# A smaller first query load, one expert unit regrouped to two output products, and a new hand-written order in an attention-and-expert kernel on one core

## The chip, the cores and the metric

The kernel runs on one core of a Trainium2 chip. The metric is the device time of one execution in microseconds. Five engines work side by side, each through its own queue in order: TensorE (PE, matmuls; its weight loads are listed as PEld), VectorE (DVE), ScalarE (ACT), GpSimd (POOL) and SyncE (SP), which issues nearly all DMAs here.

## What is computed

The first half is linear attention with sketched features, for 4 batches, 4 heads, 1088 positions and head size 32; its output, turned to 4352 tokens of 128 values, goes through an expert layer with a rational function in the place of an activation.

```python
def phi(x):
    a = np.einsum('rd,bhsd->bhsr', S1, x)          # r = 8
    b = np.einsum('rd,bhsd->bhsr', S2, x)
    return np.einsum('bhsi,bhsj->bhsij', a, b).reshape(*x.shape[:-1], r * r)
kv = np.einsum('bhsf,bhsd->bhfd', phi(k), v);  z = np.sum(phi(k), axis=2)
x = (phi(q) . kv) / (phi(q) . z + 1e-06)           # -> [4352, 128]
h = x @ w_in                                       # d_ff = 2048
P = a[0] + a[1]*h + a[2]*h*h + a[3]*h*h*h
Q = 1.0 + abs(b[0])*abs(h) + abs(b[1])*h*h
out = (P / (Q + 1e-06)) @ w_out
```

## The kernel before

**Tiling.** Keys are handled by batch (K0 to K3), each in two parts. Queries are handled in pieces of a batch (Q0.0 to Q3.2; 256 to 384 tokens each). The expert layer is cut into 21 units: each is a stretch of 256 or 512 tokens and 4, 8 or 16 of the 16 blocks of 128 hidden values, so a unit is 1024, 2048 or 4096 wide in the free dimension (all of units 3 to 17 are 4096 wide, unit 20 is 1024).

**A unit's stages.** H: matmuls h = w_in x into a PSUM tile of 1024 (two buffers). E: ACT copies it to bf16 (`hh`, three buffers). U, W, Y on DVE: |h|, |b1||h| + |b0|, and their product. P: the linear factor a3 h + a2, in halves of 2048, on ACT (`.a`) or DVE (`.d`). V on DVE: times h, which gives `g` = a3 h h + a2 h. L and X on ACT, in pieces of 2048: ln of 1 + 1e-6 + Y, and exp of its negative, which is the reciprocal `r`. S on DVE: s = h r. G on DVE: g = g s. Then three sums of output matmuls, all into one PSUM tile of a stretch: Or (w_out times a0, with r), Os (w_out times a1, with s) and Og (w_out, with g). ST transposes the finished tile on DVE, and OUT stores it. The three scaled copies of w_out are made at the start (w0 to w5, in halves).

**A query piece's stages.** T (DVE transpose), sk (sketch matmuls), c (copy out of PSUM), dw and dr (SP writes the sketches to DRAM and reads them back spread over partitions; Q0.0 and Q0.1 do without), f (DVE product), p (matmuls with the key sums `kvz`), pl, r, x (denominator plus 1e-6, reciprocal, quotient), b (transpose on PE) and kk (ACT copies into the ring `xT` that H reads). **A key batch's stages**: T0 to T2, s, c, f, p (products with v), k (copies into `kvz`).

**The order** is written out by hand in the string ORDER (L31 to L72); nothing else schedules the work. The loop at L600 runs through its steps and issues each one's instructions, so a step's place fixes its place in every engine's queue: I and F are loads issued by SP (I0 to I11 those of the start, F1.k, F1.q, F1.v and so on those of a later batch), Z is that many matmuls of zeros that fill PE's time, AB and SS prepare small constants.

**Loads of the start**, in `early` (L158): I0 and I1 keys of batch 0, I11 the second sketch matrix, I2 the first queries, I3 four loads of v, I8 the coefficients a and b, I7 the other queries of batch 0, I9 and I10 halves of w_out, I4 to I6 parts of w_in. **Names that the change touches**: `early` (L158), `a2, a3` (L240), `left`, the count of output matmuls still to come for a stretch (L456), `span`, the columns of a stage's piece (L464), `p` (L513) and the table `stages` (L596).

Of the kernel before, what the change touches and what calls it, by code (L numbers as in the profile page):

```python
# [36 lines left out]
Q0.1.kk.a V0.0 Y1.0 Q1.2.T S0.0 E2.1 G0.0 Or0.0 L1.0 U2.0 F1.v F2.k Q0.2.dr Q0.3.dw K1.p0 K1.p1 Q1.1.sk Og0.0
Q0.2.f K1.k0.a K1.k1.a Q0.2.p X1.0 Q1.1.c.a Q0.2.pl.a P2.0.a W2.0 K2.T0 K2.T1 Q0.2.r K2.T2 Q0.2.x F2.q Q1.0.dw
Os0.0 Or1.0 K2.s0 Q0.2.b Y2.0 K2.c0.a Q0.2.kk.a L2.0 K2.s1 Q2.0.T H3.0 K2.c1.a E3.0 K2.f0 V2.0 V1.0 S1.0 K2.f1
Q0.3.dr Q1.1.dw H3.1 Q1.2.sk Q2.0.sk H3.2 X2.0 Q1.2.c.a E3.1 Q1.0.dr H3.3 Q2.1.T S2.0 G2.0 Q0.3.f G1.0 E3.2  # L40
Q2.0.c.a E3.3 P3.0.a H4.0 Q0.3.p U3.0 E4.0 Q1.0.f Q0.3.pl.d W3.0 Q0.3.r Y3.0 P3.1.a H4.1 Q1.0.p Q1.0.pl.a E4.1
Q0.3.x Q1.0.r Q2.2.T Q1.0.x P4.0.d V3.0 Q1.2.dw Q2.0.dw F2.v Q1.1.dr F3.q F3.k Q2.1.sk Q2.1.c.a L3.0 H4.2 Q2.1.dw
Q1.2.dr H4.3 Q0.3.b E4.2 E4.3 Q0.3.kk.a X3.0 Q1.0.b Os2.0 Os1.0 K2.p0 Q1.0.kk.a K2.p1 Og1.0 H5.0 L3.1 U4.0 P4.1.d
W4.0 V4.0 Q1.1.f K2.k0.a X3.1 E5.0 K2.k1.a H5.1 E5.1 Y4.0 S3.0 Or2.0 Q1.1.p Og2.0 H5.2 L4.0 X4.0 Q1.2.f K3.T0 ST2
G3.0 K3.T1 Q3.0.T E5.2 L4.1 Q1.1.pl.a Q1.2.p H5.3 Q1.2.pl.a Q2.0.dr E5.3 X4.1 Q1.2.r P5.0.d Q1.1.r U5.0 Q1.1.x
W5.0 Q1.2.x Y5.0 S4.0 K3.T2 H6.0 H6.1 Q2.2.sk Or3.0 E6.0 H6.2 P5.1.a E6.1 Or4.0 H6.3 Or3.1 Q1.1.b Q2.2.c.a E6.2
L5.0 E6.3 P6.0.d Q2.0.f U6.0 V5.0 Og3.0 Q1.1.kk.a H7.0 X5.0 P6.1.a L5.1 E7.0 G4.0 W6.0 X5.1 Os3.0 H7.1 E7.1
Q3.0.sk Q2.0.p H7.2 Os4.0 H7.3 Q1.2.b Or4.1 P7.0.a E7.2 Q3.1.T Y6.0 Og4.0 H8.0 S5.0 Q2.0.pl.d V6.0 G5.0 Q3.2.T
Q2.2.dw OUT2 Q2.1.dr L6.0 Q2.2.dr E7.3 X6.0 P7.1.a Q3.0.c.a Q2.0.r U7.0 E8.0 ST4 Q2.0.x Q2.1.f W7.0 H8.1 Q1.2.kk.a
L6.1 E8.1 V7.0 Y7.0 OUT4 Q3.0.dw Q2.0.b H8.2 Q3.1.sk Q3.1.c.a Q3.1.dw Q3.0.dr Or5.0 Q2.1.p Q2.0.kk.a X6.1  # L50
Q2.1.pl.a E8.2 Q2.1.r S6.0 Q2.2.f P8.0.d L7.0 Or5.1 H8.3 K3.s0 K3.c0.a E8.3 Q2.1.x U8.0 G6.0 W8.0 H9.0 X7.0 Og5.0
H9.1 K3.f0 E9.0 Q2.1.b Q2.2.p Q2.2.pl.d H9.2 Y8.0 L7.1 E9.1 P8.1.a V8.0 H9.3 Os5.0 Or6.1 K3.s1 Or6.0 X7.1 E9.2
H10.0 Os6.0 P9.0.a E9.3 Og6.0 H10.1 S7.0 L8.0 P9.1.a K3.c1.a X8.0 U9.0 Q2.2.r Q2.1.kk.a E10.0 L8.1 E10.1 X8.1 F3.v
W9.0 Q3.0.f Q3.1.dr Q2.2.x K3.f1 Y9.0 ST6 G7.0 Q3.1.f H10.2 Or7.0 Or7.1 H10.3 Or8.1 Or8.0 E10.2 H11.0 L9.0 E10.3
V9.0 P10.0.d S8.0 U10.0 X9.0 E11.0 L9.1 H11.1 Os7.0 H11.2 K3.p0 E11.1 H11.3 K3.p1 X9.1 E11.2 W10.0 P10.1.d Y10.0
L10.0 E11.3 Os8.0 H12.0 K3.k1.a X10.0 K3.k0.a L10.1 X10.1 G8.0 V10.0 U11.0 S9.0 W11.0 G9.0 Q3.0.p Q3.2.sk Q2.2.b
Og7.0 H12.1 E12.0 Q3.0.pl.a Og8.0 P11.0.a E12.1 Q3.2.c.a P11.1.a S10.0 Q3.0.r Y11.0 ST8 Q3.0.x H12.2 H12.3 E12.2
L11.0 Or9.0 Q2.2.kk.a Q3.0.b Or9.1 E12.3 Q3.0.kk.a X11.0 Q3.2.dw OUT8 Q3.2.dr OUT6 G10.0 V11.0 U12.0 P12.0.d
Q3.1.p H13.0 Q3.1.pl.a L11.1 W12.0 P12.1.d Y12.0 Q3.1.r E13.0 X11.1 H13.1 Os9.0 Or10.1 H13.2 Or10.0 E13.1 L12.0
E13.2 S11.0 Q3.1.x V12.0 Q3.2.f G11.0 H13.3 H14.0 Q3.1.b Og9.0 Os10.0 X12.0 E13.3 U13.0 P13.0.d W13.0 L12.1 E14.0  # L60
X12.1 P13.1.a H14.1 E14.1 S12.0 Y13.0 Og10.0 ST10 H14.2 Q3.1.kk.a P14.0.a H14.3 Or11.0 Or11.1 E14.2 L13.0 E14.3
G12.0 V13.0 X13.0 U14.0 Q3.2.p Q3.2.pl.a P14.1.d Q3.2.r H15.0 E15.0 W14.0 Q3.2.x H15.1 L13.1 E15.1 X13.1 Or12.1
H15.2 Os11.0 H15.3 Or12.0 E15.2 Y14.0 V14.0 L14.0 S13.0 Og11.0 E15.3 U15.0 P15.0.d W15.0 P15.1.d Y15.0 X14.0 L14.1
H16.0 E16.0 Og12.0 H16.1 H16.2 Os12.0 X14.1 E16.1 L15.0 E16.2 P16.0.a V15.0 G13.0 ST12 S14.0 OUT10 OUT12 H16.3
Or13.0 Q3.2.b E16.3 Q3.2.kk.a Or13.1 H17.0 X15.0 E17.0 L15.1 Or14.0 H17.1 H17.2 E17.1 H17.3 Os13.0 Or14.1 X15.1
E17.2 U16.0.d P16.1.d W16.0.d G14.0 Y16.0 Og13.0 Os14.0 Og14.0 H18.0 V16.0 S15.0 L16.0 E17.3 U17.0.d P17.0.d
# [9 lines left out]
def kernel(  # L76
# [436 lines left out]
    def p(i, k, eng):  # L513
# [3 lines left out]
                                    op0=AX.mult, op1=AX.add)  # L517
        else:
            nc.scalar.activation(out=at(i, "g", *c), in_=at(i, "hh", *c), func=ACT.Identity, scale=a3, bias=a2)  # L519
# [123 lines left out]
```

## Time and profile before

| | us |
|---|---|
| runs before | 265.71, 266.57, 266.58; median 266.57 |
| profiled execution | 265.94 |
| its span, first to last instruction | 264.2 |
| evacuation E, 1024 wide, ACT (68) | 1.041 each |
| ln L / exp X, 2048 wide, ACT (32 / 32) | 1.955 / 1.951 each |
| factor P, 2048 wide, on ACT (16) / on DVE (16) | 2.120 / 0.806 each |
| product 4096 wide, DVE (60 in V, Y, S, G) | 2.281 to 2.291 each |
| output matmul 512 columns bf16, PE (eight in a row) | 1.73 |

A group's mean is the time from an instruction's start to its end as the profiler gives it. The next instruction of a full queue starts some 0.1 us before that end on ACT and DVE, and much earlier on PE, so means add up to more than the queue's time.

### The profile page before, as it was taken

To read this page: it belongs to the slowest core of one execution; us is meant where nothing else is said; L and a number is where in the kernel's file an instruction comes from. 1 tells how busy PE (TensorE), PEld (TensorE's weight loads), DVE (VectorE), ACT (ScalarE), POOL (GpSimd) and SP (SyncE) were. 2 spreads that over 40 slices of the span, in tenths; PEclk is the share of its full clock that TensorE was granted. 3 is DMA by queue.
4 is the path that set the end of the run, shared out by engine and by line. 5 is a ranking of instruction groups with operands and counts; after the bars stand their busy time and mean duration, and the time that the engine had idled before them with its cause. 6 is when DMAs were issued, how large, how long until landed. Compare 5 with 4: busy or idle time off the path is not lost.

```text
span 264.2 us, 3693 instructions
## 1 busy us (share of the span) xinstructions
PE 258.0 (98%) x1407; PEld 148.5 (56%) x1421; DVE 252.6 (96%) x238; ACT 242.3 (92%) x224; POOL 2.9 (1%) x24
## 2 busy tenths in 40 slices
PE   8999999999999999999999999999999999999994
PEld 3797855677344545555444655444544457465683
DVE  3899999999999999999999999999999999999993
ACT  2178998999999999999999999999999999999990
POOL 4000000000000000000000000000000000000000
PEclk9999999999999999999999999999999999999999
DMA  6999654793017104940000004600200020020121
GB/s 168 287 298 256 197 154 103 200 247 87 0 29 168 58 9 79 187 109 0 0 0 2 0 1 76 130 0 0 37 5 0 0 40 0 2 39 1 26 36 20
DMA packets 30784, 20.16 MB, mean 76 GB/s; under 512 B 20016, under 2 KB 26544, under 8 KB 30768
## 3 DMA queue, kind: packets, MB, share of 16 engines
q1 hardware_dynamic: 30080, 19.85, 30.8%
q8 instruction: 11, 0.18, 0.3%
q10 hardware_dynamic: 688, 0.08, 0.2%
q14 instruction: 5, 0.04, 0.1%
HBM read 16.71 MB, written 3.21 MB: 75 GB/s over the span
## 4 chain that ended last, share of the span: by engine, by line
PE 46%; ACT 25%; DVE 17%; issue 10%; DVEq 0%; ACTq 0%
PE h_ps L485 21%; PE out_ps L550 14%; ACT ln L528 7%; ACT r L532 6%; ACT hh L491 6%; ACT g L519 4%; DVE s L536 4%; DVE g L540 3%; PE att_ps L406 2%; DVE g L523 2%; PE out_ps L193 2%; DVE w L511 2%; PE att_ps L312 2%; DVE u L498 2%; PE att_ps L284 2%
## 5 line engine op out<-in xcount | busy, mean ns | idle before, releaser
L485 PE MATMUL h_ps<-xT,w_in_sb 128*128 128x512 f32 (+1 forms) x320 | 126.1, 533 | 0.1
L485 PEld LDWEIGHTS h_ps<-xT,w_in_sb 128*128 128x128 f32 x320 | 59.2, 190 | 43.5 <-issue 33.0
L550 PEld LDWEIGHTS <-w_out 128*128 128x128 bf16 x480 | 46.4, 98 | 48.3 <-issue 14.3
L491 ACT CAST hh<-h_ps 128x1024 bf16<-128x1024 f32 x68 | 70.8, 1041 | 1.8 <-PE h_ps L485 1.4
L528 ACT ACTIVATE ln<-w 128x2048 f32<-128x2048 bf16 (+1 forms) x36 | 66.8, 1856 | 0.4 <-DVE w L511 0.2
L532 ACT ACTIVATE r<-ln 128x2048 bf16<-128x2048 f32 (+1 forms) x36 | 66.7, 1852 | 0.4 <-PE out_ps L550 0.2
L536 DVE TENSOR_TENSOR s<-hh,r 128x4096 bf16<-128x4096 bf16 (+2 forms) x21 | 39.4, 1878 | 0.5 <-ACT r L532 0.4
L511 DVE TENSOR_TENSOR w<-w,u 128x4096 bf16<-128x4096 bf16 (+2 forms) x21 | 39.5, 1880 | 0.1
L540 DVE TENSOR_TENSOR g<-g,s 128x4096 bf16<-128x4096 bf16 (+2 forms) x21 | 39.4, 1878 | 0.1
L523 DVE TENSOR_TENSOR g<-g,hh 128x4096 bf16<-128x4096 bf16 (+2 forms) x21 | 39.5, 1882 | 0.0
L519 ACT ACTIVATE g<-hh,a_sb 128x2048 bf16<-128x2048 bf16 (+1 forms) x17 | 35.2, 2068 | 0.0
L550 PE MATMUL out_ps<-r,w_out 128*128 128x512 bf16 (+1 forms) x154 | 34.0, 346 | 0.5
L550 PE MATMUL out_ps<-g,w_out 128*128 128x512 bf16 (+1 forms) x158 | 32.6, 347 | 0.1
L550 PE MATMUL out_ps<-s,w_out 128*128 128x512 bf16 (+1 forms) x155 | 31.8, 346 | 0.3
L506 DVE TENSOR_SCALAR w<-u,b_abs 128x4096 bf16<-128x4096 bf16 (+2 forms) x19 | 22.6, 1187 | 0.1
L498 DVE TENSOR_SCALAR u<-hh 128x4096 uint16<-128x4096 uint16 (+2 forms) x20 | 21.0, 1048 | 0.3 <-ACT hh L491 0.3
L406 PEld LDWEIGHTS att_ps<-kvz,a_all 128*118 128x118 f32 (+2 forms) x144 | 16.8, 186 | 3.5 <-issue 1.3
L406 PE MATMUL att_ps<-kvz,a_all 128*118 128x66 f32 (+2 forms) x144 | 17.1, 268 | 0.1
L516 DVE TENSOR_SCALAR g<-hh,a_sb 128x2048 bf16<-128x2048 bf16 (+1 forms) x19 | 14.5, 762 | 0.2 <-ACT hh L491 0.2
L312 PEld LDWEIGHTS att_ps<-v_sb,k_p 128*64 128x64 f32 (+1 forms) x288 | 8.8, 138 | 2.4 <-issue 1.9
L278 DVE STREAM_TRANSPOSE kT<-k_sb 128x512 f32<-128x512 f32 (+2 forms) x12 | 6.2, 536 | 3.6 <-DMA k_sb<-in_k_dram 3.6
L391 DVE TENSOR_TENSOR a_all<-a_all,b_all 128x704 f32<-128x704 f32 (+3 forms) x11 | 9.7, 880 | 0.0
(58 smaller groups left out, 128.5 us busy)
## 6 DMA issues: line engine op xcount, KB each, us to landing
a_all<-sk_d SPq DMA_DIRECT2D x6, 352.0 KB
b_all<-sk_d SPq DMA_DIRECT2D x12, 176.0 KB
v_sb<-in_v_dram SPq DMA_DIRECT2D x12, 144.0 KB
k_sb<-in_k_dram SPq DMA_DIRECT2D x3, 544.0 KB
q_sb<-in_q_dram SPq DMA_DIRECT2D x3, 544.0 KB
a_all<-sk_d SPq DMA_DIRECT2D x3, 384.0 KB
b_all<-sk_d SPq DMA_DIRECT2D x6, 192.0 KB
ln<-in_moe_w_out_dram SPq DMA_DIRECT2D x2, 512.0 KB
```

The costliest lines, as they stand in the source:

```text
L406: nc.tensor.matmul(self.nd[:self.tl, o:o + 2 * KW], lhsT=self.group(t, c), rhs=kvz[self.b % 2][:, c, :], start=True, stop=True)
L485: nc.tensor.matmul(t[:, (x - part * m) * tl:(x - part * m + 1) * tl], lhsT=w_in_sb[:, (f0 + x) * 128:(f0 + x + 1) * 128], rhs=xT[:, p:p + ...
L491: nc.scalar.copy(out=at(i, "hh", c, ce), in_=live[i]["h", part][:, :ce - c])
L498: nc.vector.tensor_scalar(out=at(i, "u", *c).bitcast(U16), in0=at(i, "hh", *c).bitcast(U16), scalar1=0x7FFF, scalar2=None, op0=AX.bitwise_and)
L511: nc.vector.tensor_mul(out=at(i, "w", *c), in0=at(i, "w", *c), in1=at(i, "u", *c))
L519: nc.scalar.activation(out=at(i, "g", *c), in_=at(i, "hh", *c), func=ACT.Identity, scale=a3, bias=a2)
L523: nc.vector.tensor_mul(out=at(i, "g", *c), in0=at(i, "g", *c), in1=at(i, "hh", *c))
L528: nc.scalar.activation(out=t[:, :ce - c], in_=at(i, "w", c, ce), func=ACT.Ln, bias=1.0 + 1e-6)
L532: nc.scalar.activation(out=at(i, "r", c, ce), in_=live[i]["ln", k][:, :ce - c], func=ACT.Exp, scale=-1.0)
L536: nc.vector.tensor_mul(out=at(i, "s", *c), in0=at(i, "hh", *c), in1=at(i, "r", *c))
L540: nc.vector.tensor_mul(out=at(i, "g", *c), in0=at(i, "g", *c), in1=at(i, "s", *c))
L550: nc.tensor.matmul(outs[t0][:, :tl], lhsT=w_sb[y][:, f0 + x, :], rhs=at(i, "rsg"[y], x * tl, (x + 1) * tl), start=first and j == 0, stop=l ...
```

## The change

The first query load I2 takes 256 columns rather than 512, and I7 the other 832. For unit 6 (named in TWO) Os is left out: a1 is added to `g` ahead of the product with s, in a new stage A between V and G, one half on DVE and one on ACT. Since then g s = (a3 h h + a2 h + a1) h r, Og gives what Os and Og gave together. The last unit's pieces of L, X, S, G get a cap of 2048 (END). ORDER is new throughout. Beside the new places, these steps change engine: K0.c1, Q0.1.pl, W18, both halves of P9 and P11.1 go from ACT to DVE; Q0.3.pl, Q2.0.pl, Q2.2.pl, P6.0, P10.0, P15.1, P20, U20 and w1 go from DVE to ACT; U19 and W20 go from ACT to DVE, W19 from DVE to ACT; w4 and w5 change sides. I7 moves ahead of F1.k, I8 behind I9, I6 behind Q0.2.dw.

```diff
+QA = 256
+TWO = (6,)
+END = 2048
...
-            nc.sync.dma_start(out=q0[:, 0:512], in_=q0_src[:, 0:512])
+            nc.sync.dma_start(out=q0[:, 0:QA], in_=q0_src[:, 0:QA])
...
-            nc.sync.dma_start(out=q0[:, 512:S], in_=q0_src[:, 512:S])
+            nc.sync.dma_start(out=q0[:, QA:S], in_=q0_src[:, QA:S])
...
-    for t0, tl, f0, n in units:
-        left[t0] = left.get(t0, 0) + 3 * n
+    for i, (t0, tl, f0, n) in enumerate(units):
+        left[t0] = left.get(t0, 0) + (2 if i in TWO else 3) * n
...
-        w = WIDE.get(stage, 2048)
+        w = END if i == NU - 1 and stage in "LXSG" else WIDE.get(stage, 2048)
...
+    def plus(i, k, eng):
+        c = span(i, "P", k)
+        if eng == "d":
+            nc.vector.tensor_scalar(out=at(i, "g", *c), in0=at(i, "g", *c), scalar1=a1, scalar2=None, op0=AX.add)
+        else:
+            nc.scalar.activation(out=at(i, "g", *c), in_=at(i, "g", *c), func=ACT.Identity, bias=a1)
```

The start of the order, old and new:

```diff
-I0 I11 I1 I2 K0.T0 SS0 Z10 K0.s0 K0.T1 K0.c0.a K0.T2 K0.f0 Q0.0.T Z2 K0.s1 Z2 Q0.0.sk I3 Z2 K0.p0 I8 F1.k I7 I9 I4
-I6 I5 I10 K0.c1.a K0.f1 Q0.0.c.d Q0.0.f Q0.1.T K0.p1 K0.k1.d Q0.2.T K1.T0 K0.k0.a Q0.1.sk Q0.0.p Q0.2.sk K1.T1
+I0 I11 I1 I2 K0.T0 SS0 Z10 K0.s0 K0.T1 K0.c0.a K0.T2 Q0.0.T K0.f0 Z2 K0.s1 K0.c1.d I3 Z2 Q0.0.sk K0.p0 I7 F1.k I9
+I8 I4 I5 I10 K0.f1 K0.p1 Q0.0.c.d Q0.1.T Q0.0.f K0.k1.d Q0.2.T K1.T0 K0.k0.a Q0.1.sk Q0.0.p Q0.2.sk Q0.1.c.a
```

The part with the new stage (P6.0 and P6.1 stand before it), and the tail:

```diff
+P7.0.a U7.0.d A6.0.d W7.0.d Q3.0.f L6.1 Y7.0 E8.0 K3.c1.a K3.f1 X6.1 H8.1 Q3.1.sk Q3.1.c.a E8.1 A6.1.a S6.0 ST4
+H8.2 Q2.0.b Q2.1.p H8.3 G5.0 G6.0 Or5.0 Or5.1 Q2.2.p E8.2 P7.1.a P8.0.d Q2.0.kk.a E8.3 Q2.2.pl.a Q2.1.pl.a H9.0
...
-ST16 U19.0.a L18.0 Z1 Or17.0 E20.0 X18.0 P19.0.a W19.0.d G17.0 Y19.0 S18.0 U20.0.d L19.0 W20.0.a Os17.0 Or17.1
-Og17.0 OUT14 X19.0 OUT16 G18.0 ST17 P20.0.d Y20.0 V19.0 S19.0 V20.0 G19.0 L20.0 Z4 Or18.0 OUT17 X20.0 Og18.0
-Os18.0 Or19.0 Os19.0 Or20.0 Og19.0 S20.0 Os20.0 G20.0 Og20.0 ST20 OUT20
+Og16.0 Og15.0 H20.0 S17.0 W19.0.a L18.0 ST16 Y19.0 G17.0 E20.0 X18.0 U20.0.a L19.0 P19.0.a Z5 Or17.0 Or17.1 Os17.0
+OUT14 V18.0 S18.0 W20.0.d Og17.0 ST17 V19.0 Y20.0 X19.0 P20.0.a L20.0 S19.0 G18.0 V20.0 G19.0 OUT16 Z2 Or18.0
+OUT17 X20.0 Or19.0 Os18.0 Os19.0 Z1 Og18.0 S20.0 Or20.0 Og19.0 Os20.0 G20.0 Og20.0 ST20 OUT20
```

More of the change, by code (lines that the diff above doesn't have):

```diff
@@ L31 @@
 ORDER = """
-I0 I11 I1 I2 K0.T0 SS0 Z10 K0.s0 K0.T1 K0.c0.a K0.T2 K0.f0 Q0.0.T Z2 K0.s1 Z2 Q0.0.sk I3 Z2 K0.p0 I8 F1.k I7 I9 I4
-I6 I5 I10 K0.c1.a K0.f1 Q0.0.c.d Q0.0.f Q0.1.T K0.p1 K0.k1.d Q0.2.T K1.T0 K0.k0.a Q0.1.sk Q0.0.p Q0.2.sk K1.T1
-Q0.1.c.a Q0.0.pl.a Q0.0.r Q0.0.x K1.T2 K1.s0 Q0.2.c.a Q0.0.b K1.s1 Q0.1.f K1.c0.a Q0.3.T Q0.0.kk.a H0.0 w2.a K1.f0
-K1.c1.a AB0 w0.a K1.f1 w4.d E0.0 Q0.1.p H1.0 Q0.3.sk H2.0 Q0.2.dw F1.q Q0.1.pl.a w3.a E1.0 P0.0.d U0.0 w5.a W0.0
-Y0.0 Q0.1.r w1.d Q1.0.T P1.0.d U1.0 L0.0 Q0.3.c.d H2.1 X0.0 Q0.1.x W1.0 Q1.1.T Q1.0.sk Q1.0.c.a Q0.1.b E2.0
@@ L37 @@
[L37 to L66, printed above, removed]
@@ L67 @@
-W17.0.d Y17.0 ST14 X16.0 L16.1 P17.1.a X16.1 E18.0 H18.1 Or15.0 G15.0 V17.0 Or15.1 Os15.0 H19.0 Or16.1 L17.0 E18.1
-X17.0 P18.0.d U18.0.d S16.0 L17.1 W18.0.a V18.0 G16.0 Y18.0 Og15.0 Or16.0 Os16.0 Og16.0 H20.0 X17.1 E19.0 S17.0
-ST16 U19.0.a L18.0 Z1 Or17.0 E20.0 X18.0 P19.0.a W19.0.d G17.0 Y19.0 S18.0 U20.0.d L19.0 W20.0.a Os17.0 Or17.1
-Og17.0 OUT14 X19.0 OUT16 G18.0 ST17 P20.0.d Y20.0 V19.0 S19.0 V20.0 G19.0 L20.0 Z4 Or18.0 OUT17 X20.0 Og18.0
-Os18.0 Or19.0 Os19.0 Or20.0 Og19.0 S20.0 Os20.0 G20.0 Og20.0 ST20 OUT20
+I0 I11 I1 I2 K0.T0 SS0 Z10 K0.s0 K0.T1 K0.c0.a K0.T2 Q0.0.T K0.f0 Z2 K0.s1 K0.c1.d I3 Z2 Q0.0.sk K0.p0 I7 F1.k I9
@@ new lines @@
+I8 I4 I5 I10 K0.f1 K0.p1 Q0.0.c.d Q0.1.T Q0.0.f K0.k1.d Q0.2.T K1.T0 K0.k0.a Q0.1.sk Q0.0.p Q0.2.sk Q0.1.c.a
+Q0.0.pl.a Q0.2.c.a K1.T1 Q0.0.r Q0.0.x K1.T2 K1.s0 Q0.0.b K1.s1 K1.c0.a Q0.0.kk.a Q0.1.f K1.f0 Q0.3.T H0.0 AB0
+w0.a K1.c1.a w2.a E0.0 K1.f1 w5.d Q0.1.p H1.0 Q0.3.sk Q0.2.dw I6 F1.q w3.a w4.a Q0.1.pl.d P0.0.d U0.0 Q0.1.r V0.0
+Q0.1.x W0.0 Q0.3.c.d Y0.0 E1.0 H2.0 w1.a Q0.1.b E2.0 Q0.1.kk.a L0.0 P1.0.d Q1.0.T U1.0 Q1.1.T W1.0 V1.0 Y1.0 H2.1
+Q1.0.sk E2.1 X0.0 Q1.0.c.a F1.v K1.p0 K1.p1 Q0.2.dr Q1.2.T L1.0 U2.0 Q0.2.f Q0.3.dw F2.k Q0.2.p K1.k0.a K1.k1.a
@@ new lines @@
+Q0.2.pl.a S0.0 W2.0 G0.0 Q0.2.r Q0.2.x Q1.1.sk Or0.0 Os0.0 Q0.2.b Q1.2.sk Og0.0 X1.0 Q1.1.c.a Q0.2.kk.a P2.0.a
+Y2.0 S1.0 K2.T0 F2.q Q1.0.dw G1.0 H3.0 K2.s0 Q0.3.dr Q1.1.dw Q1.0.dr L2.0 Q1.2.c.a K2.c0.a E3.0 X2.0 K2.T1 Q2.0.T
+H3.1 Q2.0.sk K2.T2 Q2.1.T V2.0 K2.s1 K2.f0 Q2.2.T Q0.3.f H3.2 E3.1 K2.c1.a E3.2 H3.3 Q2.0.c.a E3.3 Q0.3.p H4.0
+Q0.3.pl.a P3.0.a E4.0 S2.0 K2.f1 G2.0 Q1.0.f U3.0.d Q1.2.dw Q1.1.dr F3.q F2.v Q2.0.dw F3.k Q1.2.dr Q0.3.r W3.0.d
+Q0.3.x Y3.0 Q1.0.p H4.1 H4.2 P3.1.a Q1.0.pl.a E4.1 L3.0 Q1.1.f Q1.0.r P4.0.d Q1.0.x V3.0 Q0.3.b H4.3 Os1.0 Or1.0
@@ new lines @@
+E4.2 Q0.3.kk.a E4.3 X3.0 Or2.0 Q1.0.b Q1.1.p Q2.1.sk Q1.0.kk.a Q1.1.pl.a L3.1 Q2.1.c.a X3.1 Q2.1.dw Q2.0.dr U4.0.d
+P4.1.d W4.0.d Q1.1.r Q2.2.sk H5.0 H5.1 Os2.0 Og1.0 E5.0 Q3.0.T Y4.0 Q1.1.x L4.0 E5.1 Q2.2.c.a H5.2 Q3.0.sk Og2.0
+H5.3 E5.2 Q3.0.c.a X4.0 H6.0 S3.0 Q1.2.f V4.0 G3.0 E5.3 L4.1 E6.0 X4.1 U5.0.d P5.0.d ST2 Q2.0.f W5.0.d Q2.2.dw
+S4.0 P5.1.a Y5.0 V5.0 Q1.1.b K2.p0 K2.p1 H6.1 Or3.0 H6.2 E6.1 Q1.1.kk.a P6.0.a K2.k0.a H6.3 Q1.2.p K2.k1.a Or3.1
+Q2.0.p Q3.0.dw Q2.1.dr G4.0 Q2.1.f Q3.1.T E6.2 Q1.2.pl.a L5.0 E6.3 Q1.2.r Q2.0.pl.a Q2.0.r U6.0.d X5.0 Or4.1 H7.0
@@ new lines @@
+Os3.0 K3.T0 Or4.0 H7.1 K3.s0 W6.0.d K3.T1 Q1.2.x Y6.0 Q3.2.T P6.1.a E7.0 V6.0 L5.1 OUT2 Q2.2.dr Q3.0.dr E7.1 H7.2
+Og4.0 Q1.2.b H7.3 K3.c0.a X5.1 E7.2 L6.0 S5.0 Q2.2.f K3.T2 K3.f0 Q2.0.x Og3.0 Os4.0 H8.0 K3.s1 Q1.2.kk.a E7.3 X6.0
+P7.0.a U7.0.d A6.0.d W7.0.d Q3.0.f L6.1 Y7.0 E8.0 K3.c1.a K3.f1 X6.1 H8.1 Q3.1.sk Q3.1.c.a E8.1 A6.1.a S6.0 ST4
+H8.2 Q2.0.b Q2.1.p H8.3 G5.0 G6.0 Or5.0 Or5.1 Q2.2.p E8.2 P7.1.a P8.0.d Q2.0.kk.a E8.3 Q2.2.pl.a Q2.1.pl.a H9.0
+Og6.0 H9.1 F3.v Q3.1.dw Q3.1.dr OUT4 U8.0.d V7.0 W8.0.d Q2.1.r Q2.2.r Og5.0 L7.0 E9.0 P8.1.a X7.0 E9.1 L7.1 H9.2
@@ new lines @@
+H9.3 Os5.0 E9.2 Or6.1 H10.0 Or6.0 Y8.0 P9.0.d V8.0 Q3.1.f Q2.2.x X7.1 E9.3 S7.0 U9.0.d Q2.1.x P9.1.d W9.0.d ST6
+G7.0 V9.0 Y9.0 L8.0 E10.0 X8.0 H10.1 Q2.1.b H10.2 E10.1 L8.1 Q2.1.kk.a E10.2 K3.p0 H10.3 X8.1 P10.0.a E10.3 L9.0
+S8.0 H11.0 K3.p1 Q3.2.sk Or7.0 Or7.1 E11.0 H11.1 U10.0.d X9.0 K3.k0.a K3.k1.a E11.1 L9.1 Or8.1 Os7.0 H11.2 Q2.2.b
+E11.2 X9.1 H11.3 Og7.0 G8.0 W10.0.d P10.1.d Y10.0 V10.0 S9.0 E11.3 P11.0.a Q3.2.c.a L10.0 U11.0.d Q3.0.p Q2.2.kk.a
+Q3.0.pl.a Or8.0 H12.0 Q3.1.p X10.0 Q3.1.pl.a G9.0 Q3.0.r P11.1.d W11.0.d Q3.0.x Y11.0 V11.0 H12.1 Os8.0 Og8.0
@@ new lines @@
+Q3.0.b L10.1 E12.0 X10.1 ST8 E12.1 S10.0 Q3.1.r P12.0.d Q3.1.x L11.0 H12.2 H12.3 Or9.0 E12.2 Q3.0.kk.a E12.3 Or9.1
+H13.0 X11.0 E13.0 OUT6 Q3.2.dw OUT8 Q3.2.dr L11.1 H13.1 E13.1 X11.1 Or10.1 H13.2 Os9.0 H13.3 Q3.1.b Or10.0 U12.0.d
+E13.2 H14.0 P12.1.d W12.0.d V12.0 Y12.0 S11.0 G10.0 L12.0 E13.3 X12.0 H14.1 Og9.0 E14.0 L12.1 E14.1 Q3.1.kk.a
+X12.1 H14.2 Os10.0 U13.0.d G11.0 Og10.0 H14.3 W13.0.d P13.0.d Q3.2.f Y13.0 P13.1.a E14.2 L13.0 E14.3 P14.0.a S12.0
+ST10 G12.0 H15.0 Or11.0 Or11.1 E15.0 X13.0 H15.1 Q3.2.p E15.1 Q3.2.pl.a L13.1 H15.2 Or12.0 Or12.1 Os11.0 H15.3
@@ new lines @@
+E15.2 X13.1 U14.0.d V13.0 W14.0.d Q3.2.r P14.1.d Q3.2.x Y14.0 V14.0 S13.0 L14.0 Q3.2.b E15.3 U15.0.d H16.0 X14.0
+Q3.2.kk.a E16.0 Og11.0 H16.1 H16.2 Os12.0 Og12.0 G13.0 W15.0.d P15.0.d Y15.0 L14.1 E16.1 X14.1 P15.1.a E16.2 S14.0
+ST12 H16.3 P16.0.a E16.3 L15.0 H17.0 Or13.0 E17.0 Or13.1 H17.1 Os13.0 H17.2 OUT10 OUT12 G14.0 U16.0.d P16.1.d
+W16.0.d V15.0 V16.0 Y16.0 X15.0 E17.1 L15.1 E17.2 X15.1 Or14.0 H17.3 Or14.1 H18.0 Og13.0 Os14.0 Og14.0 E17.3 L16.0
+H18.1 S15.0 U17.0.d G15.0 W17.0.d ST14 Y17.0 X16.0 E18.0 L16.1 X16.1 E18.1 L17.0 Or15.0 Or15.1 H19.0 Or16.1 Os15.0
@@ L72 @@
+Or16.0 P17.0.d U18.0.d S16.0 X17.0 P17.1.a W18.0.d L17.1 E19.0 G16.0 Y18.0 V17.0 U19.0.d P18.0.d X17.1 Os16.0
+Og16.0 Og15.0 H20.0 S17.0 W19.0.a L18.0 ST16 Y19.0 G17.0 E20.0 X18.0 U20.0.a L19.0 P19.0.a Z5 Or17.0 Or17.1 Os17.0
+OUT14 V18.0 S18.0 W20.0.d Og17.0 ST17 V19.0 Y20.0 X19.0 P20.0.a L20.0 S19.0 G18.0 V20.0 G19.0 OUT16 Z2 Or18.0
+OUT17 X20.0 Or19.0 Os18.0 Os19.0 Z1 Og18.0 S20.0 Or20.0 Og19.0 Os20.0 G20.0 Og20.0 ST20 OUT20
 """
@@ L239 @@
     ab0, ab1 = b_abs[:, 0:1], b_abs[:, 1:2]
-    a2, a3 = a_sb[:, 2:3], a_sb[:, 3:4]
+    a1, a2, a3 = a_sb[:, 1:2], a_sb[:, 2:3], a_sb[:, 3:4]
     w_sb = [big.tile([128, nf, d_model], BF, name=f"w_out_{i}") for i in range(3)]
@@ L595 @@
     queries = [[Queries(b, y) for y in range(len(CUTS[b]) - 1)] for b in range(B)]
-    stages = {"H": hidden, "E": evac, "U": d_abs, "W": d_w, "Y": d_y, "P": p, "V": d_hp, "L": a_ln, "X": a_exp,
+    stages = {"H": hidden, "E": evac, "U": d_abs, "W": d_w, "Y": d_y, "P": p, "A": plus, "V": d_hp, "L": a_ln, "X": a_exp,
               "S": d_s, "G": d_g, "Or": lambda i, k: gather(i, 0, k), "Os": lambda i, k: gather(i, 1, k),
```

## The prediction

> **What bounds the kernel now.** I read the page's busy times first, then busy time by stretch of the span, then the chain of work that ended last, the waits, and at last the timeline of the first 20 us and of the last 28.
>
> ```profile
> PE 258.0 (98%) x1407; PEld 148.5 (56%) x1421; DVE 252.6 (96%) x238; ACT 242.3 (92%) x224; POOL 2.9 (1%) x24
> ...
> 0.00:20.00 20.00, 18.77 (x172) 13.74 (x173) 13.84 (x27) 7.24 (x17) 2.94 (x24) 1.00 0.88 251
> 20.00:40.00 20.00, 19.95 (x174) 14.04 (x172) 19.86 (x35) 18.85 (x27) 0.00 (x0) 1.00 0.71 198
> 40.00:60.00 20.00, 20.00 (x152) 12.38 (x151) 19.71 (x22) 18.91 (x22) 0.00 (x0) 1.00 0.72 185
> ...
> 160.00:200.00 40.00, 39.78 (x147) 19.51 (x149) 39.60 (x30) 40.00 (x34) 0.00 (x0) 1.00 0.21 40
> 200.00:240.00 40.00, 39.81 (x168) 23.19 (x170) 39.82 (x27) 39.68 (x29) 0.00 (x0) 1.00 0.09 14
> ```
>
> The columns of the stretches are length, then busy time of PE, PEld, DVE, ACT and POOL, the granted clock, and DMA. From 20 to 240 us all three engines are full; the three busy columns sum to 219 of 220 us for PE and DVE and 217 for ACT. The 92% of ACT on the page is an average: ACT is short of work only before 20 us, between 20 and 60 us (2.2 us idle) and in the tail. So no single engine bounds this kernel, and an edit that unloads one and loads another is worth what the fullest engine afterwards allows.
>
> ```profile
> 85.05 0.90 ACT hh L491
> 85.95 1.81 ACT r L532
> ...
> 118.77 1.99 ACT g L519
> ...
> 149.08 2.20 DVE s L536
> ...
> 187.75 1.73 PE out_ps L550 x8
> ```
>
> These pieces of the chain (start, length, what) give what an instruction costs in a full queue, start to start: 0.90 us for an evacuation E, 1.81 for each L and X, 2.00 for a linear factor P on ACT, 2.20 for a 4096-wide product on DVE, 1.73/8 = 0.216 us for an output matmul. The group means are 0.1 us longer on ACT and DVE, since neighbours overlap. The chain runs on ACT from 52 to 124 us, on DVE to 160, on PE to 225, and on DVE again: it changes hands because all are full.
>
> ```profile
> ACT hh L491 <- PE h_ps L485: 1.4, 3, 0.5
> ...
> ACT sk_sb L253 <- DMA a_all<-sk_d: 0.4, 1, 0.4
> ...
> ACT r L532 <- PE out_ps L550: 0.2, 1, 0.2
> ACT ln L528 <- DVE w L511: 0.2, 1, 0.2
> ```
>
> After 20 us ACT waits six times, 2.2 us in all (total, times, longest). A wait also loses the 0.1 us overlap, 0.6 more; three gaps under 0.1 us make it about **3.1 us** that ACT could still win.
>
> **The change, part by part.**
>
> *First query load (I2) of 256 tokens.* 128 KiB (131 KB) less stand ahead of the four v loads.
>
> ```profile
> 10.04 2.18 PEld L312 LDWEIGHTS att_ps<-v_sb,k_p 128*64 128x64 f32 x72 [0.42 <-DMA v_sb<-in_v_dram]
> ...
> 12.47 0.39 DVE L255 COPY kvz<-att_ps 64x33 f32<-64x33 f32 x2 [0.98 <-PE att_ps L312]
> ...
> 15.90 0.27 ACT L253 COPY b_sk<-att_ps 128x128 f32<-128x128 f32 x1 [0.76 <-PE att_ps L284]
> ```
>
> The key products K0.p0 wait for v at 10.04, and DVE and ACT wait behind them (the brackets). DMA moved 210 to 364 GB/s between 5 and 8 us, so 131 KB are worth 0.36 to 0.62 us if they count in full and 0 if v is limited otherwise; the wait seen is only 0.42, but the matmuls Z2 that go from just ahead of it add as much slack again. I take **0.35 us**. K0.p1 needs K0.f1 on DVE, which moves from 9.81 to about 10.1, since K0.c1 (0.3 us) goes ahead of it from ACT to DVE; p1 starts at 10.7, so that copy is free, and ACT idled 1.35 us before it anyway. Then Q0.1.sk, Q0.0.p and K1.s0 follow without a gap as before, and ACT begins its full stretch with K1.c0 at 15.55, not 15.90. The other 832 columns (I7) are now queued right behind v and ahead of the next keys: 426 KB at those rates land 1.2 to 2.0 us after v, 10.9 to 11.7; Q0.1.T is due on DVE at 10.8. DVE had 0.98 us of waiting before the kvz copy, which covers most of that; at the late end the 0.35 is gone. The third part of w_in (I6) now goes behind Q0.2.dw on SP, so it is issued at about 15.5; the first key load, 256 KB, took 3.0 us from its issue at 0.73 to its reader at 3.77, so 512 KB at 0.25 MB/us take some 4.0 and land near 19.5; H2.0 reads them at 21. Behind the dw on SP stand only I6 and the load of q for batch 1, whose reader Q1.0.T comes at 23.
>
> *Unit 6.* Os6 goes: 8 output matmuls of 512 columns, 8 x 0.216 = **-1.73 us on PE**. A6.0 on DVE adds one pass of 2048: the nearest row is the factor P on DVE, 0.72 start to start (0.81 by its group), **+0.72**. A6.1 on ACT adds one like P on ACT, **+2.00**. No row shows the add alone; by bounds it is at most P's 2.1 and at least the ln's 1.81 of the same width. Both stand between V6 and G6; A6.0 waits for nothing new (same engine), A6.1 waits for V6 on DVE, which by the sums below ends 12 us ahead. Behind A6.1 on ACT stands E8.2, and behind that the buffer of H9.0 on PE, and U8 on DVE, which has S6, G5, G6 and P8 ahead of it.
>
> *Linear factors and other swaps.* P6.0, P10.0, P15.1 go to ACT and both of P9 and P11.1 to DVE as counts: equal. P20 goes to ACT (+1.13 there, -0.42 on DVE), W18 to DVE (-1.98 ACT, +0.72 DVE), one w_out part to ACT (+1.05, -0.62), two denominators to ACT net (+0.15, -0.25). END changes nothing: the last unit is 1024 wide, under both caps. Z: two fillers fewer early, three more in the tail, all in PE's waiting.
>
> Sums: **PE -1.73, DVE +0.15, ACT +2.00 + 1.13 - 1.98 + 1.05 + 0.15 = +2.35 us.** The change takes from PE and gives to ACT. ACT's last instruction, X20, ended at 258.15, and S20, G20, Og20, the last transpose and the stores follow it in both orders. So with every wait kept, X20 moves by -0.35 + 2.35 = +2.0; with every wait gone by 2.0 - 3.1 = -1.1, and a little more: where an X stands right behind its own L, an L right behind an X, or DVE has U, W, Y or S, G of one unit in a row, the trace shows about 0.13 us extra each; the new order has three such places fewer on ACT and six fewer on DVE, **-0.35** on ACT.
>
> *Which waits stay with the new order?* I added the start-to-start times along each engine's new order up to each hand-over. ACT's sum comes first to E3.3, 0.9 us ahead of its matmuls, and to L3.0 at 46.7 us, while Y3 ends on DVE at 47.8: **0.9 to 1.1 us** of waiting by then, one time, not 3.1. From there on PE (unloaded) is 0 to 5 us ahead of ACT at each hand-over, and DVE not over 0.1 us behind once ACT has lost that 1 us. The same sums for the old order put ACT 2 us ahead of PE at E4.3 and 2 us ahead of DVE at Y4: it waits there in the trace. So ACT: -0.35 + 2.35 - 3.1 + 0.95 - 0.35 = **-0.5 us**; I take **-0.6**, the small hand-overs of the tail being better spaced as well. DVE would allow -0.4 + 0.15 less its later waits (1.1 us) and six of the 0.13: -2. PE would allow -2.1. ACT decides.
>
> [...]
>
> **The sum**: span 264.2 - 0.6 = 263.6; with the 1.74 us that the profiled execution (265.94) has beyond its span, **265.3 us**. The profiled one lies 0.6 under the median of the runs (266.57), within their spread, so I keep its scale and let the range take that in.
>
> **Rivals.**
>
> *PE's saving is paid in full.* PE is 98% busy, and the chain stays on PE for 60 us on end (164 to 225). Then the time falls by 1.73 + 0.35: 263.9. Against it: ACT is as full from 60 to 240 us (39.97, 39.83, 40.00 of 40) and is given 2.35 us. [...] The row of 1.73 us for eight matmuls, back to back, says that this trace's PE is in fact full.
>
> *ACT becomes the bound and keeps its waits.* A6.1 and P20 sit in ACT's queue, and the hand-overs make it wait as often as before: X20 moves by +2.0, 267.9. It is slower than before from the point where ACT's waiting after 15.5 us exceeds 1.4 us (the sum's 0.95 plus some 0.5). For it: ACT waited 3.1 us in the old order. Against: most of that was on PE, which now runs ahead.
>
> *The smaller load does not bring v earlier*, because v is limited by its own small rows or the 832 columns crowd it: -0.6 + 0.35 = -0.25, 265.7.
>
> **How the numbers follow.** Chances: forecast 0.45, PE paid in full 0.22, ACT with its waits 0.18, no earlier v 0.15. 0.5% is 1.33 us, about what a measurement of this kernel can tell from no change. The PE rival and the forecast's lower end (0.06) lie below that: faster 0.28. Four fifths of the ACT rival lie above it: slower 0.15. The rest is 0.57. The range goes from the PE rival to just short of the ACT rival, 263.8 to 267.6; the unknown ends (v's 0 to 0.62, the add's 1.8 to 2.1, the median's 0.6) lie inside.
>
> **What would show it.** Right: K0.p0 at 9.5 to 9.8 and K1.c0 at 15.5 in the timeline; ACT about 244.4 us busy, PE 1.7 less; ACT's waits on PE gone after 50 us, and one wait near L3.0 of about a us; DVE idle more often for ACT than before. Wrong: ACT's waits sum to over 2 us, or the products of DVE that read X wait for it again and again, so that DVE's idle time grows; or K0.p0 still at 10.0.

## The result, and the profile after

The changed kernel is slower, by half a per cent: 267.47 us median (266.51 to 269.25, 12 runs) against 266.42 (265.55 to 266.65, 12 runs), ratio 1.0049 with a 95% interval of 1.003 to 1.0068. Its profiled execution took 267.07 us, with a span of 265.3. The forecast was 265.3, a little faster; the time lies inside its range, on the other side.

First the page's busy times of the changed kernel, then its stretches of the span (columns as in the prediction: length, then PE, PEld, DVE, ACT, POOL, granted clock, DMA share, GB/s).

```profile
PE 256.8 (97%) x1399; PEld 148.1 (56%) x1414; DVE 252.8 (95%) x237; ACT 242.8 (92%) x227; POOL 2.9 (1%) x24
```

```profile
0.00:20.00 20.00, 18.81 (x171) 14.31 (x172) 14.33 (x30) 7.05 (x15) 2.94 (x24) 1.00 0.81 219
20.00:40.00 20.00, 18.23 (x164) 12.80 (x163) 18.01 (x35) 17.85 (x25) 0.00 (x0) 1.00 0.83 231
40.00:60.00 20.00, 19.96 (x99) 12.05 (x99) 19.70 (x21) 18.95 (x23) 0.00 (x0) 1.00 0.72 165
...
160.00:200.00 40.00, 39.32 (x137) 18.35 (x139) 39.99 (x30) 39.97 (x33) 0.00 (x0) 1.00 0.15 32
200.00:240.00 40.00, 39.84 (x167) 23.20 (x169) 39.77 (x27) 39.91 (x29) 0.00 (x0) 1.00 0.09 14
```

One stretch differs: from 20 to 40 us PE lost 1.72 us against before, DVE 1.85, ACT 1.00. Everywhere else the three are nearly as full as they were (PE has less to do). A loss on three engines at once is not an engine that became the bound; all wait for something else. The waits of the changed kernel from 20 to 60 us (total, times, longest) name it:

```profile
PE att_ps L315 <- DMA sk_d<-sk_sb: 1.3, 1, 1.3
...
DVE qT L343 <- DMA q_sb<-in_q_dram: 1.1, 1, 1.1
...
DVE a_all L394 <- DMA b_all<-sk_d: 0.8, 1, 0.8
```

None of these was there before. They are batch 1's queries (Q1.0.T at 24.62 us, before 22.86), the key products K1.p0 (27.58, before 26.84; they read v of batch 1, while the profile names the last DMA that ended ahead of them), and the sketches read back for Q0.2.f. In e3 below, whose loads are those of the changed kernel, the same wait is put down to v itself:

```profile
PE att_ps L315 <- DMA v_sb<-in_v_dram: 1.8, 1, 1.8
```

What the DMA engines did meanwhile, in three stretches, before:

```profile
13.30:16.60 3.30, 3.30 (x31) 3.01 (x30) 2.88 (x8) 1.73 (x6) 0.00 (x0) 1.00 1.07 363
16.60:20.00 3.40, 3.40 (x23) 3.17 (x23) 3.25 (x4) 3.30 (x7) 0.00 (x0) 1.00 0.78 228
...
24.00:28.00 4.00, 4.00 (x57) 3.02 (x57) 3.96 (x10) 3.55 (x6) 0.00 (x0) 1.00 0.65 167
```

and after:

```profile
13.30:16.60 3.30, 3.30 (x32) 3.06 (x30) 2.88 (x7) 1.84 (x7) 0.00 (x0) 1.00 0.80 231
16.60:20.00 3.40, 3.40 (x23) 3.14 (x23) 3.40 (x6) 3.30 (x5) 0.00 (x0) 1.00 0.59 141
...
24.00:28.00 4.00, 2.67 (x27) 1.86 (x27) 3.38 (x8) 4.00 (x6) 0.00 (x0) 1.00 1.05 203
```

The last three columns tell it: from 13 to 20 us the transfers have holes (GB/s 231 and 141, before 363 and 228), since the 512 KB of I6 are not yet issued; then from 24 to 28 us they are full (1.05) with what should have come earlier, and PE is idle for 1.33 us. SyncE's part of the timeline after (start, length, engine, line) shows the order of issues:

```profile
15.06 1.76 SPq L376 DMA_DIRECT2D sk_d<-sk_sb  x2
16.86 0.58 SPq L175 DMA_DIRECT2D w_in_sb<-in_moe_w_in_dram  x1
17.77 0.33 SPq L133 DMA_DIRECT2D q_sb<-in_q_dram  x1
18.20 1.82 SPq L139 DMA_DIRECT2D v_sb<-in_v_dram  x4
```

### The profile page after: what moved, and what is told of

It reads as the page before. It is cut to its first block, busy times and chain, and to the rows that moved or that the text cites. A ratio compares the mean times of both kernels' runs of the same rounds, so it can differ in the third digit from the quotient of the medians.

```text
span 265.3 us, 3686 instructions
## 1 busy us (share of the span) xinstructions
PE 256.8 (97%) x1399; PEld 148.1 (56%) x1414; DVE 252.8 (95%) x237; ACT 242.8 (92%) x227; POOL 2.9 (1%) x24
## 3 DMA queue, kind: packets, MB, share of 16 engines
HBM read 16.71 MB, written 3.21 MB: 75 GB/s over the span
## 4 chain that ended last, share of the span: by engine, by line
DVE 39%; ACT 32%; issue 12%; PE 12%; DMA 4%; DVEq 0%; SPq 0%; ACTq 0%
DVE g L550 8%; ACT ln L538 8%; ACT r L542 8%; ACT hh L494 8%; DVE w L514 6%; DVE s L546 6%; ACT g L522 5%; DVE g L533 5%; DVE u L501 4%; DVE w L509 4%; DMA v_sb<-in_v_dram 3%; PE h_ps L488 3%; DVE g L519 2%; PE out_ps L196 2%; DVE out_sb L567 2%
## 5 line engine op out<-in xcount | busy, mean ns | idle before, releaser
L488 PE MATMUL h_ps<-xT,w_in_sb 128*128 128x512 f32 (+1 forms) x320 | 127.7, 533 | 0.5 <-ACT hh L494 0.5
L488 PEld LDWEIGHTS h_ps<-xT,w_in_sb 128*128 128x128 f32 x320 | 58.4, 190 | 41.2 <-issue 30.9
L494 ACT CAST hh<-h_ps 128x1024 bf16<-128x1024 f32 x68 | 72.4, 1064 | 1.2 <-PE h_ps L488 1.0
L542 ACT ACTIVATE r<-ln 128x2048 bf16<-128x2048 f32 (+1 forms) x36 | 67.6, 1879 | 0.1
L522 ACT ACTIVATE g<-hh,a_sb 128x2048 bf16<-128x2048 bf16 (+1 forms) x18 | 37.0, 2056 | 0.0
L560 PE MATMUL out_ps<-r,w_out 128*128 128x512 bf16 (+1 forms) x152 | 32.8, 346 | 0.7 <-DVE out_sb L567 0.2
L560 PE MATMUL out_ps<-s,w_out 128*128 128x512 bf16 (+1 forms) x148 | 30.3, 344 | 0.2
L509 DVE TENSOR_SCALAR w<-u,b_abs 128x4096 bf16<-128x4096 bf16 (+2 forms) x20 | 23.3, 1163 | 0.0
L519 DVE TENSOR_SCALAR g<-hh,a_sb 128x2048 bf16<-128x2048 bf16 (+1 forms) x18 | 13.7, 762 | 0.0
L315 PE MATMUL att_ps<-v_sb,k_p 128*64 128x64 f32 (+1 forms) x288 | 9.5, 224 | 1.3 <-DMA sk_d<-sk_sb 1.3
```

What stands on the lines that cost most here:

```text
L488: nc.tensor.matmul(t[:, (x - part * m) * tl:(x - part * m + 1) * tl], lhsT=w_in_sb[:, (f0 + x) * 128:(f0 + x + 1) * 128], rhs=xT[:, p:p + ...
L494: nc.scalar.copy(out=at(i, "hh", c, ce), in_=live[i]["h", part][:, :ce - c])
L509: nc.vector.tensor_scalar(out=at(i, "w", *c), in0=at(i, "u", *c), scalar1=ab1, scalar2=ab0, op0=AX.mult, op1=AX.add)
L542: nc.scalar.activation(out=at(i, "r", c, ce), in_=live[i]["ln", k][:, :ce - c], func=ACT.Exp, scale=-1.0)
L560: nc.tensor.matmul(outs[t0][:, :tl], lhsT=w_sb[y][:, f0 + x, :], rhs=at(i, "rsg"[y], x * tl, (x + 1) * tl), start=first and j == 0, stop=l ...
```

## The experiments

**Theories.** L (late load): the third part of w_in behind Q0.2.dw takes the transfers' time from batch 1's q, v and sketches. Rivals: A (ACT): the additions and P20 on ACT make the loss; O (order): the new hand-overs do; F (first load): the cut of the first query load does. All ratios below are to the kernel before, run on the same chip (266.19 to 266.27 us median).

**e1, the load back at its early place, all else as changed.**

```diff
-I8 I4 I5 I10 K0.f1
+I8 I4 I6 I5 I10 K0.f1
...
-Q0.2.dw I6 F1.q
+Q0.2.dw F1.q
```

> The changed kernel with one load put back: the third part of w_in (I6) is issued ahead of I5 again, not behind Q0.2.dw. Theory 1 (the late I6 stands ahead of batch 1's q and v in the DMA queues, and their readers wait): the waits of 1.1 us before Q1.0.T on DVE, 1.3 us before K1.p0 on PE and 0.8 us before Q0.2.f on DVE go, some 1 to 2 us of time comes back: 265.5 to 266.6 us, ratio to the kernel before 0.996 to 1.001. Theory 2 (ACT's added work of unit 6 and of P20 costs the time): nothing changes, 267.3 to 267.6, ratio 1.003 to 1.006. Theory 3 (the smaller first load and its crowding of v cost it): nothing changes either.

Measured: 265.38 us, ratio 0.9964 (0.9951 to 0.9977). The late load is worth 1.0049 - 0.9964 = 0.85%, 2.3 us, and without it the change is a gain. In the traces the two kernels part before 36 us (E3.0 at 37.70 and 35.88) and then run in parallel to X20 (258.19 and 256.30). Of these 1.8 us, 0.68 are there at K1.c0 already (15.79 and 15.11), ahead of the late load; the last section comes back to that. e9 below is the cleaner pair: its trace starts like that of the changed kernel (K1.c0 at 15.80), has E3.0 at 35.88, and its span is 2.0 us shorter.

**e2, the kernel before with nothing but that load moved behind Q0.2.dw.**

```diff
-I6 I5 I10
+I5 I10
...
-H2.0 Q0.2.dw F1.q
+Q0.2.dw I6 H2.0 F1.q
```

> The kernel before with one load moved alone: I6 issued behind Q0.2.dw (which stands ahead of H2.0 in the text here, so that H2.0 can read it). Theory 1: waits for batch 1's q, v and the spread sketches appear as in the changed kernel, +1 to +2 us, ratio 1.003 to 1.008. Theories 2 and 3: ratio 1.000, at most 0.001 off.

Measured: 268.07 us, ratio 1.006 (1.0037 to 1.0083). The old order shows the same wait, here as its line of the timeline:

```profile
25.36 0.58 DVE L340 STREAM_TRANSPOSE qT<-q_sb 128x384 f32<-128x384 f32 x1 [1.60 <-DMA q_sb<-in_q_dram]
```

With e1 this settles L against A, O and F as the cause of the loss: it goes and comes with this load, whatever the order.

**e5, the load at another early place, behind the second half of w_out** (`I8 I4 I5 I10 I6 K0.f1`).

> The changed kernel with I6 issued right behind I10, the second half of w_out. With I6 ahead of I5 (e1) w5 on DVE waited 1.0 us for that half and w3 on ACT 0.3. If DMA order in the first 20 us is the whole matter, these waits go and batch 1's q and v still come in time: ratio to the kernel before 0.993 to 0.997. If H2.0 or batch 1's loads become late again instead: 0.997 to 1.000.

Measured: 265.04 us, ratio 0.9954 (0.994 to 0.9968). Busy times for the stretch that had the hole, 15 to 17.5 us, after and then e5:

```profile
15.00:17.50 2.50, 2.50 (x22) 2.45 (x22) 2.50 (x5) 1.74 (x6) 0.00 (x0) 1.00 0.41 113
```

```profile
15.00:17.50 2.50, 2.50 (x21) 2.42 (x21) 2.50 (x5) 1.92 (x6) 0.00 (x0) 1.00 1.10 351
```

**e9, 448 KB of it early, 64 KB late: bytes or the place on SyncE?** (`I10 I6` with 896 columns, `Q0.2.dw I12 F1.q` with the last 128.)

```diff
-            c, e = ((0, 512), (512, 1024), (1024, d_ff))[n - 4]
+            c, e = ((0, 512), (512, 1024), (1024, d_ff - 128))[n - 4]
...
+        elif n == 12:
+            nc.sync.dma_start(out=w_in_sb[:, d_ff - 128:], in_=moe_w_in[:, d_ff - 128:])
```

> The changed kernel with 896 of the 1024 columns of the third part of w_in loaded early, right behind I10, and only the last 128 columns (64 KB) as a load of its own behind Q0.2.dw, where the changed kernel has all 512 KB. If the bytes standing ahead of batch 1's q, v and sketches make the loss, an eighth of them is left, some 0.2 us of loading, and the time is as with the whole part early: ratio to the kernel before about 0.996 (265.0 to 265.4 us), and Q1.0.T waits for q no longer than 0.2 us. If it is the place on SP (one more issue of 0.6 to 0.9 us ahead of F1.q, so that q and v are issued later), the loss stays in the main: ratio 1.001 to 1.005, with waits for q and v of batch 1 of about 1 us each.

Measured: 264.41 us, ratio 0.9935 (0.9922 to 0.9948), faster than the 0.996 expected and the fastest version of the study; its interval overlaps e5's, and the profiled spans are 263.3 and 263.2, so the two are not told apart. SyncE's part of the timeline of e9, and the transpose that reads q:

```profile
17.24 0.59 SPq L179 DMA_DIRECT2D w_in_sb<-in_moe_w_in_dram  x1
...
17.93 0.38 SPq L133 DMA_DIRECT2D q_sb<-in_q_dram  x1
18.40 1.80 SPq L139 DMA_DIRECT2D v_sb<-in_v_dram  x4
...
23.46 0.57 DVE L345 STREAM_TRANSPOSE qT<-q_sb 128x384 f32<-128x384 f32 x1
```

Here q and v are issued 0.2 us later than in the changed kernel (17.93 and 18.40, against 17.77 and 18.20), and yet the transpose starts without a bracket: it does not wait. So it is the bytes ahead in the transfers, not the moment of issue.

**e12, q of batch 1 ahead of the late load** (`Q0.2.dw F1.q I6`).

> The changed kernel with the load of q for batch 1 ahead of the third part of w_in, both still behind Q0.2.dw: only v of batch 1 and the sketches written and read back stay behind the 512 KB. If the late q (a wait of 1.1 us at Q1.0.T on DVE) makes the loss, the ratio falls to about 0.997. If the late v and sketches make it (1.3 us on PE, 0.8 on DVE), it stays at 1.003 to 1.005 with the wait of K1.p0 at about 1.3 us, and Q1.0.T no longer waits. If both have a share, 0.999 to 1.002.

Measured: 266.54 us, ratio 1.0025 (1.0002 to 1.0048), between the cases named, and its interval overlaps that of the changed kernel. Q1.0.T no longer waits for q, but my expectation that v or the sketches would then be left was wrong: the next to be late is the load itself.

```profile
PE h_ps L488 <- DMA w_in_sb<-in_moe_w_in_dram: 1.6, 1, 1.6
...
DVE qT L343 <- PE att_ps L350: 1.5, 1, 1.5
```

H2.0 (L488) waits 1.6 us for w_in. In the orders tried, with the 512 KB issued at about 17 us, some reader waits; the order behind that point chose which.

**e7 and e3, three products for unit 6 again**, in e1 and in the changed kernel (`TWO = ()`, A6.0 and A6.1 out, Os6.0 ahead of H9.0).

> As e1, with unit 6 back at three output products and without A6.0 and A6.1. If ACT decides, as the forecast said, 2.0 us less on ACT make it as fast as e1 or faster: ratio 0.990 to 0.997. If PE is the bound and its saving is paid in full, 1.73 us more on PE: ratio 1.001 to 1.004. If all three share it, in between.

Measured: e7 266.30 us, ratio 1.0005 (0.9996 to 1.0014).

> The changed kernel with unit 6 back at three output products: A6.0 and A6.1 left out, Os6.0 put in ahead of Og6.0, all else as in the changed kernel. Theory 1: about unchanged, ratio 1.002 to 1.006, since PE gets 1.7 us more and ACT 2.0 us less and the early waits stay. Theory 2: 2 us less on ACT show in the time, ratio 0.997 to 1.000. Theory 3: unchanged.

Measured: e3 268.78 us, ratio 1.0096 (1.0063 to 1.0129). Both times the two products are worth some 1.1 to 1.3 us (1.0005 - 0.9964 = 0.41%, 1.0096 - 1.0049 = 0.47%, the latter with wide intervals), though ACT has 2 us more to do. e6 below, which is e1 but for the first load and ran on e7's chip, has 0.9965. A is out. The busy times from 100 to 140 us of e7 and then of e1 show how that goes:

```profile
100.00:140.00 40.00, 40.00 (x217) 20.21 (x216) 38.57 (x29) 37.32 (x34) 0.00 (x0) 1.00 0.16 34
```

```profile
100.00:140.00 40.00, 40.00 (x216) 19.88 (x214) 39.91 (x29) 40.00 (x36) 0.00 (x0) 1.00 0.16 34
```

Without the additions the new order is bound by PE (40.00) from 100 to 140 us, and leaves DVE 1.43 and ACT 2.68 us idle there. The additions, 0.7 on DVE and 2.0 on ACT, fill just these gaps. e7 also says that the new order alone, with its swaps, the smaller first load and w_in loaded where e1 has it, is worth nothing that shows (1.0005). That puts rival O out.

**e10, the two products in the old order** (A6.0 behind V6.0, A6.1 behind X6.1 and so between E8.1 and E8.2 as in the new order, Os6.0 out).

> The kernel before with its own order and loads, only unit 6 with two output products: Os6.0 goes, A6.0 on DVE stands right behind V6.0, A6.1 on ACT right behind X6.1. PE has 1.73 us less, DVE 0.72 and ACT 2.0 more. If PE is the bound and about half of its saving reaches the end, as under the new order with the early load, the ratio is about 0.997 (0.9 us less, 265.3). If ACT decides, as the prediction had it, the time grows by what ACT's waits do not take in: 0 to 2 us, ratio 1.000 to 1.008. If the saving shows only with an order made for it, the ratio is 0.999 to 1.003.

Measured: 268.58 us, ratio 1.0093 (1.008 to 1.0107). The same edit loses 2.5 us here, a little beyond the upper end that "ACT decides" gave. The stretch from 100 to 140 us, before and then e10, and the line of e10's timeline where it breaks:

```profile
100.00:140.00 40.00, 39.84 (x162) 20.28 (x164) 39.66 (x31) 40.00 (x35) 0.00 (x0) 1.00 0.28 59
```

```profile
100.00:140.00 40.00, 36.79 (x146) 18.39 (x145) 38.59 (x30) 40.00 (x34) 0.00 (x0) 0.96 0.32 62
```

```profile
130.99 2.46 PE L488 MATMUL h_ps<-xT,w_in_sb 128*128 128x512 f32 x4 [2.90 <-ACT hh L494]
```

ACT had no gap in this stretch (40.00 before too). The addition runs on it from 104.93 us, its queue stays full, and 24 us later an evacuation comes so late that PE stands still for 2.90 us; what PE saved in matmuls is idle time. That it is the addition's 2 us that make this evacuation late is read from the full queue; no run tests it alone.

**e11, a second unit (10) with two products, on top of e5** (`TWO = (6, 10)`, Os10.0 out, A10.0 behind V10.0, A10.1 between X10.1 and E12.1).

> The changed kernel with I6 right behind I10 (ratio 0.9954 before), and unit 10 with two output products as well: Os10.0 goes, A10.0 on DVE behind V10.0, A10.1 on ACT behind X10.1. PE loses another 1.73 us, DVE gains another 0.72, ACT another 2.0. If PE still bounds after the first unit, another 0.5 to 0.9 us go: 264.2 to 264.6. If the three engines are level after the first unit, nothing is left to win and the additions count: 265.0 to 266.0. If ACT decides in full, 266 to 267.

Measured: 268.21 us, ratio 1.007 (1.0044 to 1.0097), 3 us slower than e5 and worse than any theory gave. Where e5 is level, ACT takes the addition ahead of E12.1 and PE waits:

```profile
158.22 1.99 ACT L529 ACTIVATE g<-g,a_sb 128x2048 bf16<-128x2048 bf16 x1
...
160.11 1.00 ACT L494 CAST hh<-h_ps 128x1024 bf16<-128x1024 f32 x1
...
161.16 3.66 PE L488 MATMUL h_ps<-xT,w_in_sb 128*128 128x512 f32 x4 [2.40 <-ACT hh L494]
```

**e8, the ACT half of the addition on DVE** (e1 with `A6.1.d`).

> As e1, with the second half of the addition, A6.1, on DVE (about 0.72 us) rather than on ACT (about 2.0 us). If ACT decides: 0.3 to 1 us faster than e1, ratio 0.992 to 0.995. If DVE decides: 0.5 to 0.8 us slower than e1, ratio 0.998 to 1.000. If PE does: as e1, 0.9964.

Measured: 265.51 us, ratio 0.9974 (0.9962 to 0.9985), not to be told from e1's 0.9964 (0.9951 to 0.9977). From 100 to 140 us PE is as full here as in e1 (39.98 of 40 us) and ACT idles 1.89: that fits PE as the bound.

**e4 and e6, the first query load at 512 tokens again** (`QA = 512`), in the changed kernel and in e1.

> The changed kernel with the first query load back at 512 columns and the second at 576, in the new places and order. Theory 1: the early start moves by 0 to 0.3 us, ratio 1.004 to 1.007. Theory 2: the same. Theory 3: the time comes back, ratio 0.999 to 1.001.

> As e1 (I6 early), with the first query load back at 512 columns. If the first load holds v back and v holds the start back, K0.p0 moves from 9.25 to about 10 us and the whole by 0.3 to 0.8 us: ratio 0.998 to 1.000. If v is not on the path: as e1, 0.995 to 0.997.

Measured: e4 267.32 us, ratio 1.004 (1.0019 to 1.0061), beside 1.0049 with 256; e6 265.29, ratio 0.9965 (0.9952 to 0.9978), beside 0.9964. In neither place does the smaller load change the time by anything that shows, so F is out as the cause of the loss too.

It does show in the start. K1.c0 begins between 15.90 and 16.71 us in the five kernels with 512 tokens and between 15.00 and 15.82 in the nine with 256. e1 and e6 differ in this load alone, and their first key matmuls took the same 1.00 us; here is K1.c0 of e1 (start, length, what, and in brackets the idle time ahead), then of e6:

```profile
15.11 0.27 ACT L256 COPY b_sk<-att_ps 128x128 f32<-128x128 f32 x1 [0.76 <-PE att_ps L287]
```

```profile
15.95 0.27 ACT L256 COPY b_sk<-att_ps 128x128 f32<-128x128 f32 x1 [0.76 <-PE att_ps L287]
```

By E3.0 the lead of 0.84 us has shrunk to 0.14 (35.88 and 36.02). In e1 the scaled copy w5 on DVE waits 0.95 us for its half of w_out and starts at 19.50; in e6 it does not wait and starts at 19.31. Whether the lead would last with w_in at e5's place, where w5 does not wait either, no run tests. A wait of K0.p0 for v does not tell the two loads apart: the profile shows one of 0.33 to 0.76 us on its weight loads in before, e4 and e6 with 512 tokens, and of 0.33 to 0.44 in e7, e8 and e12 with 256.

## Why the prediction was wrong

The account by ratios: late load +0.85%, two products -0.41%, everything else +0.05%; together +0.49%, 1.3 us.

- **The step that failed is the one on I6**, costed at nothing. "Behind the dw on SP stand only I6 and the load of q for batch 1, whose reader Q1.0.T comes at 23": the working asked when I6's own reader comes (H2.0, which in the changed kernel did not wait) and saw q queued behind, but priced neither the time that 512 KB take from q, v and the sketches, nor the idle transfers ahead of it. By its own figure of 0.25 MB/us it was some 2 us; the runs give 1.6 (e2) to 2.5 us (e5). I6 was also issued at 16.86, not 15.5, since it stood behind both writes of the dw.
- **"ACT decides" was wrong as a statement on the cause.** ACT's added 2.0 us went into 2.68 us in which it waited for PE from 100 to 140 us. The forecast of -0.6 is near what e1 gives (-0.4%, 1.0 us), but by two misses that cancel: from K1.c0 to X20 e5's ACT worked 238.55 us against 237.99 before, +0.56 where +2.0 was summed (2.35 less the 0.35 for neighbours), and idled 1.94 against 3.20, -1.26 where about -2.15 was (3.1 less 0.95). The swaps were not priced too high by much: start to start in the two timelines, A6.1 took 1.91 us, P20 1.13, W18 gave back 1.98, and all of them make some +2.1. What was missed is that the work common to both came closer together, by some 1.5 us where the sum had 0.6 for lost overlaps and 0.35 for neighbours: 68 evacuations at 0.897 us instead of 0.906 and 32 long pieces of X at 1.819 instead of 1.835 are most of it. That its waits on PE would end after 50 us was right (ACT is idle 0.3 us from 60 to 240 us in e1), but little hung on it: before, it had waited for PE only 0.2 us there.
- **PE's saving paid in full** was nearer to the mechanism, but about 1.1 of 1.73 us came through: e7 against e1 says that PE did bound.
- **The addition on ACT** is the longer one (2.11 us in e1, against 0.74 each on DVE in e8), but moving it to DVE won no time that shows (e8, 0.9974 beside 0.9964): from 100 to 140 us ACT had the larger gap (2.68 us against DVE's 1.43, e7).
- **The first load**: the 0.35 us were there at the start (0.84 between e6 and e1) but did not reach the end (e4, e6). In the profiled execution of the changed kernel little of it is left at K1.c0 (15.79 against 15.90 before); its first key matmuls took 0.58 us longer.
- **The signs named beforehand**, in the changed kernel: K0.p0 at 9.93 us (9.5 to 9.8 was said), ACT busy for 242.8 us (244.4), PE 1.2 less (1.7). The wait of some 0.95 us that the sum kept came as two of 0.48 for PE, at E3.2 and E3.3 (42.11 and 43.83): that term was right.
- **Rivals**: none was the cause. The slow one had a time near the result, by ACT's waits, which the traces of the changed kernel do not show; the range had been stretched towards it, so that the time lies inside it is luck.
